# Loading the keys and queries of granule 5 ahead of the values of granule 4

## Chip, cores and metric

One core of one Trainium2 chip. The metric is device time in microseconds (us) of one execution, lower is better. A profile's span is about 1.8 us shorter than the time of the same execution. The runs of the kernel before that were known at the start spread over 0.57 us (208.49 to 209.06).

## The reference

Attention (4 batches, 8 heads, 768 positions, head size 64; each query sees 8 global keys and the last 96) followed by a two-layer block with a squared ReLU:

```python
scores = q @ k.T / sqrt(D) + bias;  a = softmax(where(keep, scores, -1e9))
x = (a @ v) -> (3072, 512)
out = (s * relu(x @ w_in)**2 + b) @ w_out        # d_ff = 2048
```

Keys, queries and values come in float32. The kernel works in bf16.

## The kernel before

The work is cut into 12 granules of 256 positions, three to a batch. A granule goes through loads, transposes of keys and queries, scores, exponential and mask, the value product, and the two layers. From granule 4 on the transposes are DMA transposes, issued by SyncE; the float32 loads, which cast to bf16, are issued by GpSimd (but for the first few of the opening). In the cuts below, the lines that work out `b`, `g` and `sb` are left out too.

```python
def load_qk(j, i):                      # block i: one load of keys, one of queries
    for n in range(2):
        nc.gpsimd.dma_start(nat_tile(j)[:, n, i, :, :], rows_of(srcs[n], b, g * GB + i))

def load_v(j, blocks=range(GB)):
    for i in blocks:
        nc.gpsimd.dma_start(vbuf[b % 2][:, sb, :, 0:D], rows_of(v, b, sb))
...
def qk_by_dma(j):                       # 4 transposes: block 0 keys, queries, block 1 keys, queries
    for i in range(GB):
        for n in range(2):
            nc.sync.dma_start_transpose(qk_of(b, n)[:, g * GB + i], nat[j][:, n, i, :, :]...)
...
warm(9, 4 * P)                          # opening: idle matmuls, so that TensorE's clock rises
...
warm(4)
qk_first(1, 0, cp)
...
    for i in range(GB):
        load_qk(4, i)
    load_v(3)
    load_v(4)
    load_granule(5)                     # k, q, k, q, v, v
...
qk_by_dma(4)
load_scalars()                          # two tiny loads, also on SyncE
...
qk_by_dma(5)
...
make_voff(4)                            # VectorE: reads values of 3 and block 0 of 4
...
step(8, [lambda: rest(2, 0)] + late_p1(3, (0,)), late_p1(3, (1, 2)), late_p1(3, (3,)))
step(9, p2[2][1:2], late_p1(3, (4, 5)), late_p1(3, (6, 7)))   # begins with granule 5's first scores
```

The softmax here doesn't subtract the row's maximum and nothing guards it: scores larger than these inputs give would overflow.

## Time and profile before

| | kernel before |
|---|---|
| time, first three runs | 208.49, 208.91, 209.06 us |
| time of the profiled execution | 209.15 us |
| span of the profile | 207.4 us |
| TensorE busy | 202.1 us (97%) |

With TensorE busy for 97% of the span, its own waits are the place to look.

### The profile page before, as it was taken

What the parts mean: (1) busy time and instruction counts of PE and PEld (TensorE: products, weight loads), DVE (VectorE), ACT (ScalarE), POOL (GpSimd) and SP (SyncE); (2) the same over time, 40 slices, a digit from 0 to 9 for tenths busy, and PEclk for the clock granted to TensorE, in tenths of its full rate; (3) what the DMA queues carried; (4) which work ended last, traced back from release to release, by engine and by line L of the source; (5) the groups of instructions that cost most, each with busy time, mean ns of one, the idle gap of its engine ahead of it and who ended that gap; (6) DMA issues with size and microseconds to landing.
All of it is one profiled execution on the core that took longest, in us unless ns stands there. A gap on an engine that the chain in (4) does not pass through costs nothing.

```text
span 207.4 us, 5323 instructions
## 1 busy us (share of the span) xinstructions
PE 202.1 (97%) x2191; PEld 160.1 (77%) x2191; DVE 161.3 (78%) x338; ACT 128.5 (62%) x198; POOL 68.9 (33%) x90
## 2 busy tenths in 40 slices
PE   7999999999999999999999999999999999999993
PEld 2678884557867485878888898888888889888883
DVE  7786599977989856799799974699866696737974
ACT  5875669486976548786664595663695764476200
POOL 8985333799365300810900828200000000000000
PEclk9999999999999999999999999999999999999999
DMA  5999999999999999999999999999570300240006
GB/s 164 172 179 202 207 206 177 155 152 129 110 150 120 151 132 218 155 213 212 152 198 153 125 154 178 194 172 126 52 206 0 95 14 0 56 150 0 0 9 196
DMA packets 110836, 28.17 MB, mean 136 GB/s; under 512 B 97852, under 2 KB 109308, under 8 KB 110812
## 3 DMA queue, kind: packets, MB, share of 16 engines
q0 software_dynamic: 76000, 13.11, 90.1%
q1 hardware_dynamic: 33612, 14.13, 41.7%
q10 hardware_dynamic: 1200, 0.59, 1.1%
q8 instruction: 17, 0.28, 0.6%
q14 instruction: 7, 0.06, 0.1%
HBM read 27.26 MB, written 6.29 MB: 162 GB/s over the span
## 4 chain that ended last, share of the span: by engine, by line
PE 65%; DMA 23%; POOL 9%; issue 1%; DVE 0%; POOLq 0%
PE ps L619 29%; PE ps L819 24%; DMA nat<-in_q_dram 12%; DMA w_in_bf<-in_moe_w_in_dram 6%; PE ps L667 5%; DMA qx<-nat 4%; PE ps_s L441 4%; PE ps_av L495 3%; POOL vb L108 3%; POOL nat L102 3%; POOL w_in_bf L140 2%; POOL nat L116 1%; PE ps_last L819 0%; DVE o_last L828 0%; POOL rel L173 0%
## 5 line engine op out<-in xcount | busy, mean ns | idle before, releaser
L619 PE MATMUL ps<-xT,w_in_bf 128*128 128x256 bf16 x768 | 90.3, 273 | 0.0
L629 ACT ACTIVATE gT<-ps 128x512 bf16<-128x512 f32 x96 | 55.8, 599 | 46.8 <-PE ps L619 46.6
L619 PEld LDWEIGHTS <-w_in_bf 128*128 128x128 bf16 x768 | 73.0, 98 | 9.4 <-DVE xT L594 0.2
L450 ACT ACTIVATE pt<-ps_s 128x1024 bf16<-128x1024 f32 (+1 forms) x44 | 39.3, 946 | 3.3 <-PE ps_s L441 3.3
L667 PE MATMUL ps<-w_out_bf,gT 128*128 128x512 bf16 x128 | 29.7, 380 | 0.0
L457 DVE TENSOR_TENSOR pt<-pt,tmpl 128x1024 bf16<-128x1024 bf16 (+1 forms) x40 | 24.6, 645 | 3.8 <-ACT pt L450 3.7
L819 PEld LDWEIGHTS <-gsum 128*128 128x128 bf16 x256 | 24.1, 98 | 3.7 <-DVE gsum L782 0.5
L108 POOL DMA_DIRECT2D vb<-in_v_dram x24 | 21.4, 906 | 6.9 <-DMA w_out_bf<-in_moe_w_out_dram 3.4
L793 DVE TENSOR_TENSOR gT<-gT 128x1024 bf16<-128x1024 bf16 x20 | 13.7, 686 | 11.7 <-ACT gT L629 11.7
L667 PEld LDWEIGHTS <-gT 128*128 128x128 bf16 x128 | 11.7, 98 | 13.0
L466 DVE TENSOR_TENSOR xn<-ps_av,rc 128x256 bf16<-128x256 f32 x48 | 20.4, 425 | 1.7
L819 PEld LDWEIGHTS <-gT 128*128 128x128 bf16 x200 | 18.6, 98 | 2.3
L465 DVE RECIPROCAL rc<-ps_av 128x4 f32<-128x4 f32 x48 | 8.6, 179 | 12.3 <-PE ps_av L495 10.4
L116 POOL DMA_DIRECT2D nat<-in_k_dram x16 | 14.2, 885 | 9.2 <-DMA nat<-in_k_dram 5.1
L495 PEld LDWEIGHTS <-pt 128*128 128x128 bf16 x320 | 14.4, 97 | 2.7 <-DVE xn L466 0.7
L632 DVE TENSOR_TENSOR gT<-gT 128x512 bf16<-128x512 bf16 x32 | 13.0, 422 | 3.5 <-ACT gT L629 3.3
L495 PE MATMUL ps_av<-vb,pt 128*128 128x65 bf16 x208 | 15.5, 193 | 0.0
L819 PE MATMUL ps<-w_out_bf,gsum 128*128 128x256 bf16 x128 | 15.3, 273 | 0.0
L116 POOL DMA_DIRECT2D nat<-in_q_dram x16 | 14.2, 888 | 2.9 <-DMA w_in_bf<-in_moe_w_in_dram 1.9
L819 PE MATMUL ps<-wsub,gsum 128*128 128x256 bf16 x128 | 15.1, 273 | 0.0
L819 PE MATMUL ps<-w_out_bf,gT 128*128 128x256 bf16 x120 | 13.9, 273 | 0.0
L122 POOL COPY gate<-xT 1x1 bf16<-1x1 bf16 x6 | 1.1, 176 | 35.9 <-DMA xT<-xn 35.9
(112 smaller groups left out, 228.5 us busy)
## 6 DMA issues: line engine op xcount, KB each, us to landing
out_dram<-o_q SPq DMA_DIRECT2D x15, 256.0 KB, 2.6
vb<-in_v_dram POOLq DMA_DIRECT2D x24, 128.0 KB, 8.3
nat<-in_k_dram POOLq DMA_DIRECT2D x22, 128.0 KB, 7.7
nat<-in_q_dram POOLq DMA_DIRECT2D x22, 128.0 KB, 7.6
w_out_bf<-in_moe_w_out_dram POOLq DMA_DIRECT2D x4, 512.0 KB, 16.2
w_in_bf<-in_moe_w_in_dram POOLq DMA_DIRECT2D x4, 256.0 KB, 7.4
w_in_bf<-in_moe_w_in_dram POOLq DMA_DIRECT2D x2, 512.0 KB, 11.3
out_dram<-o_sb SPq DMA_DIRECT2D x4, 256.0 KB, 6.3
```

The costliest lines, as they stand in the source:

```text
L108: nc.gpsimd.dma_start(vbuf[b % 2][:, sb, :, 0:D], rows_of(v, b, sb))
L116: nc.gpsimd.dma_start(t[:, n, i, :, :], rows_of(srcs[n], b, sb))
L450: nc.scalar.activation(pt[:, :, 0:ncol], ps[:, :, 0:ncol], ACT.Exp, scale=QSCALE)
L457: nc.vector.tensor_tensor(pv, pv, m.rearrange("p h a c -> p h (a c)"), ALU.mult)
L466: nc.vector.tensor_tensor(dst, av[:, :, :, 0:D], rc[:].to_broadcast((P, 2, 2, D)), ALU.mult)
L495: nc.tensor.matmul(av[:, i, hi, 0 : D + 1], lhsT=pt[:, hi, c * P : (c + 1) * P], rhs=vv, start=(n == 0), stop=(n == len(terms) - 1),)
L619: nc.tensor.matmul(ps[:, i, :], lhsT=w_in_bf[:, kc, fc * P : (fc + 1) * P], rhs=xT[j][:, kc, :], start=(kc == 0), stop=(kc == KC - 1),)
L629: nc.scalar.activation(gs, ps[:], ACT.Relu)
L632: nc.vector.tensor_tensor(gs, gs, gs, ALU.mult)
L667: nc.tensor.matmul(po[:], lhsT=g_of(j)[:, fc, tb * P : (tb + 1) * P], rhs=w_out_bf[:, fc, :], start=(fc == 0), stop=(fc == FC - 1),)
L793: outs.append(lambda: nc.vector.tensor_tensor(gs, gs, gs, ALU.mult))
L819: nc.tensor.matmul(ps[:, tb, cs], lhsT=stat[:, fc, tb * P : (tb + 1) * P], rhs=mov[:, fc, cs], start=(fc == 0), stop=(fc == NH - 1),)
```

## The change

Intent: granule 5's keys and queries need a DMA transpose after their load, the values of granule 4 do not. So let the loads with the longer way go first. The number of loads and their sizes are the same.

```diff
     for i in range(GB):
         load_qk(4, i)
     load_v(3)
+    for i in range(GB):
+        load_qk(5, i)
     load_v(4)
-    load_granule(5)
+    load_v(5)
```

## The prediction

> **What bounds the kernel now.** I read the page first: which engine is full, and what the chain that ended last consists of.
>
> ```profile
> PE 202.1 (97%) x2191; PEld 160.1 (77%) x2191; DVE 161.3 (78%) x338; ACT 128.5 (62%) x198; POOL 68.9 (33%) x90
> PE 65%; DMA 23%; POOL 9%; issue 1%; DVE 0%; POOLq 0%
> ```
>
> TensorE has work for 202.1 of the 207.4 us span. The chain is TensorE in its last part and transfers in its first. I therefore asked what TensorE itself waited for in the whole execution. Two answers came, one of them in the opening:
>
> ```profile
> PE ps_w L161 <- DVE idle L151: 1.2, 1, 1.2
> PE ps_s L441 <- DMA qx<-nat: 0.5, 1, 0.5
> ```
>
> So one wait on a transfer exists after the opening, 0.5 us long. The chain in order of time says where it is:
>
> ```profile
> 48.56 11.61 DMA nat<-in_q_dram
> 60.17 0.02 issue
> 60.19 8.86 DMA qx<-nat
> 69.06 0.04 issue
> 69.10 0.57 PE ps_s L441 x14
> 69.66 3.56 PE ps L667 x16
> ```
>
> Read it downwards: a load of queries issued at 48.56 lands at 60.17. At once a DMA transpose of that block is issued. It lands at 69.06, and the score matmuls start 0.04 us later. From there to 204 us the chain is TensorE without a transfer. By the program's order these are the scores of the first two units of granule 5: scores(8) and scores(9), of granule 4, stand at 59.06 and 62.00, and each later step issues the next. The load is the last of the four that granule 5's keys and queries need, its query block 1.
>
> TensorE's timeline sizes the stall:
>
> ```profile
> 68.36 0.23 PE L441 MATMUL ps_s<-qx,kx 64*128 64x128 bf16 x2
> 69.10 0.34 PE L441 MATMUL ps_s<-qx,kx 64*128 64x128 bf16 x6 [0.51 <-DMA qx<-nat]
> 69.26 0.40 PE L441 MATMUL ps_s<-qx,ko 64*128 64x128 bf16 x8
> 69.60 3.63 PE L667 MATMUL ps<-w_out_bf,gT 128*128 128x512 bf16 x16
> ```
>
> Two score matmuls (block 0) run at 68.36, then nothing until block 1 is there. From the first of these 16 matmuls to the next group is 69.60 - 68.36 = 1.24 us. The same 16 undisturbed, of the next step, go from 77.13 to 77.69: 0.56 us. The stall is really 1.24 - 0.56 = 0.68 us; the 0.51 is less because the second matmul's modelled end is counted into the busy time.
>
> The order of the loads is seen in GpSimd's timeline:
>
> ```profile
> 42.35 3.51 POOL L108 DMA_DIRECT2D vb<-in_v_dram  x4
> 45.87 0.89 POOL L116 DMA_DIRECT2D nat<-in_k_dram  x1
> 46.74 0.89 POOL L116 DMA_DIRECT2D nat<-in_q_dram  x1
> 47.61 0.90 POOL L116 DMA_DIRECT2D nat<-in_k_dram  x1
> 48.56 0.88 POOL L116 DMA_DIRECT2D nat<-in_q_dram  x1
> 49.43 1.77 POOL L108 DMA_DIRECT2D vb<-in_v_dram  x2
> ```
>
> The four at 42.35 are the values of granules 3 and 4, then come keys and queries of 5, then its values. Issue plus time to landing, read for each issue alone, gives: values of 4 at 44.08 + 6.0 = 50.1 and 44.95 + 7.0 = 52.0; granule 5's keys and queries at 55.9, 57.3, 58.0 and 60.2.
>
> **What the Trainium skill says.** "DMA: Bandwidth & Descriptors", section "Queues, rings and completion order": an engine consumes a ring's descriptors in ring order, and goes round-robin between queues. The loads above do land in the order of issue, so a load moved forward should take the landing slot of the one it passes. The same page, "Issuing engines are not separate DMA queues": transfers issued from all engines interleave on the same 16. The trace agrees: from 55 to 59 us and from 60.5 to 68 us the transposes share with the loads, at 145 and 132 GB/s for both together. "Perfetto Trace Analysis", section "DMA Instruction — SWDGE (GPSIMD)": the profiled window of such an issue is descriptor generation, not the movement. Here it is 0.88 us against 6 to 14 us to landing, so what counts is the landing slot and not the 2 x 0.88 us of issue. The same page, "Tensor Engine Instruction (MATMUL, LD_WEIGHTS)": matmul ends are estimated, which is why I size the stall from starts.
>
> **The change part by part.** Nothing is added or removed: 14 loads of 128 KB stay, four of them pass two others. Issue work and bytes are equal.
>
> *Keys and queries of 5 go forward by two slots.* In the old slots the four would land at 50.1, 52.0, 55.9 and 57.3 instead of 55.9, 57.3, 58.0 and 60.2. SyncE issues their transposes in program order, after those of granule 4 and two small loads, the second of which runs from 52.08 to 53.57:
>
> ```profile
> 52.08 1.49 SPq L168 DMA_DIRECT2D b_bc<-in_moe_b_dram  x1
> 55.92 1.20 SPq L360 DMA_TRANSPOSE kx<-nat  x1
> 57.32 1.19 SPq L360 DMA_TRANSPOSE qx<-nat  x1
> 58.61 1.35 SPq L360 DMA_TRANSPOSE kx<-nat  x1
> 60.19 1.54 SPq L360 DMA_TRANSPOSE qx<-nat  x1
> ```
>
> Each of the four now waits for its load. With the change the first can go at 53.6 (held by SyncE, no longer by its load), the second at 54.9, the third at 56.2, the fourth at about 57.6 (its load lands at 57.3). The fourth is 60.2 - 57.6 = 2.6 us earlier. With 8.9 us to landing it would land at 66.5. Granule 4's last transpose lands at 49.41 + 9.7 = 59.1, and transposes go through in order; so I allow a further 0.5 to 1 us and say 66.5 to 67.5. TensorE asks at about 68.4. The stall of 0.68 us goes, and the rest of the 2.6 us is slack.
>
> *Values of 4 go back by four slots.* Their new slots are 58.0 and 60.2, perhaps 1 to 1.5 us later, as transposes will now run beside loads in 59 to 60.5, where loads had the engines alone. That makes about 59 and 61.5. The first reader of block 0 is VectorE's copy into the off-diagonal values at 62.31, of block 1 the value matmuls at 65.16. Slack is about 3 us for each, so this costs nothing.
>
> *What follows.* From 69.1 on everything TensorE does moves forward by what the stall gives up. The next transfers it needs are granule 6's transposes, issued 65.37 to 70.70, with the known landings at 73.9 and 77.6; their scores are due at 81.8 and would then be due at 81.1. Loads behind the reordered group keep their slots. I find no wait to give the time back.
>
> Sum: -0.68 us at most, -0.6 expected. 208.91 - 0.6 = 208.3 us.
>
> **The rivals.**
> 1. *The stall moves to granule 4.* Its last transpose lands at 59.1 and TensorE starts scores(8) at 59.06, so that one has no slack. If granule 5's transposes, issued 2.3 us earlier, slow it by half a microsecond, the gain is lost there: 208.8. For it: both share the engines with loads. Against it: granule 4's are issued by 51.4, ahead in the same queue. I give it 1 in 5.
> 2. *The transposes are bound by themselves.* If granule 5's cannot start until 60 us for a reason other than their issue, the landing stays at 69 and the time at 208.9. For it: latency of 8.4 to 9.7 us is far above 1.2 us of issue, so something queues. Against it: the first of granule 6 took some 7 us with the same load, and granule 5's issue is plainly bound by its loads. 1 in 8.
> 3. *The values of 4 come late.* If the landing slips beyond 62.3, VectorE stalls, its masks come later, and the value matmuls at 65.16 may too; a slip of 4 us would cost about 0.5 us, 209.3 or so. 3 us of slack speak against it. 1 in 20.
> 4. *More is gained than the stall.* TensorE is without a gap afterwards, so no.
>
> **Range and chances.** The three runs of before spread by 208.49 to 209.06, 0.6 us, as much as the gain. With rival 1 or 2 above and a good run below, 207.8 to 208.9 should hold 8 in 10. A gain of over 2% would be 4.2 us, six times the only stall to be had; a loss of that size would need several transfers to miss their users by microseconds. Both are near nothing.
>
> **What would show it.** In the changed profile, TensorE's wait on the transposed queries should be gone, the 16 score matmuls near 68.4 should take 0.56 us, the four transposes of 5 should start near 53.6, and the copy of the off-diagonal values should not wait for a load. I am wrong if a wait of TensorE stands at 59 us, if one remains near 68.4, or if VectorE waits for the values of granule 4. Then the chain would again show a transfer just ahead of TensorE, at another place.

## The result, and the profile after

| | before | after |
|---|---|---|
| median of the same rounds | 208.72 us (208.49 to 209.06, 4 runs) | 208.81 us (208.60 to 208.93, 4 runs) |
| ratio | | 1.0002 (0.9983 to 1.0021) |
| span of the profile | 207.4 us | 207.1 us |

A ratio is the mean time of one kernel's fast runs over that of the other's of the same rounds, so not quite the ratio of the medians quoted. The result is inside the range of the prediction, near its upper end; the gain of 0.6 us is not there.

The wait itself is gone. All waits of TensorE in the profile after:

```profile
PE ps_w L161 <- DVE idle L151: 1.2, 1, 1.2
PE ps_s L441 <- ACT qx L331: 0.3, 1, 0.3
PE ps L667 <- issue: 0.2, 1, 0.2
```

None is for a transfer. TensorE's timeline after, at granule 5's first scores:

```profile
68.83 0.40 PE L441 MATMUL ps_s<-qx,kx 64*128 64x128 bf16 x8
69.06 0.39 PE L441 MATMUL ps_s<-qx,ko 64*128 64x128 bf16 x8
69.38 3.63 PE L667 MATMUL ps<-w_out_bf,gT 128*128 128x512 bf16 x15
```

The 16 score matmuls take 69.38 - 68.83 = 0.55 us, as predicted, where they took 1.24 us. But they begin at 68.83 and not at 68.36: TensorE is 0.47 us late when it gets there. So the next group starts only 69.60 - 69.38 = 0.22 us earlier than before, and the spans differ by about as much (207.1 against 207.4 us).

How the loads moved, from GpSimd's timeline after:

```profile
42.06 1.77 POOL L108 DMA_DIRECT2D vb<-in_v_dram  x2
43.79 0.91 POOL L102 DMA_DIRECT2D nat<-in_k_dram  x1
44.66 0.92 POOL L102 DMA_DIRECT2D nat<-in_q_dram  x1
45.52 0.94 POOL L102 DMA_DIRECT2D nat<-in_k_dram  x1
46.40 0.94 POOL L102 DMA_DIRECT2D nat<-in_q_dram  x1
47.26 3.61 POOL L108 DMA_DIRECT2D vb<-in_v_dram  x4
```

With the times to landing of these issues (6.0, 6.8, 7.6 and 10.3 us), keys and queries of 5 land at 49.8, 51.5, 53.1 and 56.7 us; the two value loads of granule 4 land at 47.26 + 10.2 = 57.5 and 48.24 + 11.2 = 59.4. SyncE's timeline after shows the transposes of granule 5:

```profile
52.41 2.27 SPq L360 DMA_TRANSPOSE kx<-nat  x1
54.78 1.22 SPq L360 DMA_TRANSPOSE qx<-nat  x1
56.10 1.32 SPq L360 DMA_TRANSPOSE kx<-nat  x1
57.52 2.05 SPq L360 DMA_TRANSPOSE qx<-nat  x1
```

The last lands 8.9 us after its issue, at 66.4, which is 2.4 us ahead of the matmuls.

Where, then, were the 0.47 us lost? Ahead of anything that the change touches, in the opening. TensorE's timeline of the kernel before, and then that of the changed one, at the first four bias matmuls:

```profile
5.85 0.81 PE L416 MATMUL ps_s<-open_bf 128*128 128x384 bf16 x4
```

```profile
6.13 1.32 PE L416 MATMUL ps_s<-open_bf 128*128 128x384 bf16 x4
```

These are the same four matmuls at the same place, before any load of granule 4 or 5 is issued: 0.81 us in one execution and 1.32 in the other. The traces' records of the granted clock explain it: full speed begins at 5.14 us in the one and at 7.15 us in the other. The page's clock row shows tenths of full speed in slices of 5 us and has 9 from its first slice in both, so one does not see it there. The Trainium skill, "TensorE: Matmul & The Clock Gate", section "What's actually happening", says that the clock rises after some 3.4 us of activity, counted in a free-running window, and is therefore "run-variable". The traces agree that it varies: in eleven further ones below, all of kernels with these nine idle matmuls, the rise is between 4.0 and 6.8 us. With TensorE's first matmul at 1.2 us, the earliest rise came after 2.8 us of work, not 3.4.

At its scores near 9 us the changed kernel is 9.55 - 8.86 = 0.69 us behind. The kernel before then loses some 0.2 us of that lead on the way to 68 us, 0.1 of it at scores(8), which take 59.73 - 59.06 = 0.67 us there and 0.56 in the changed kernel.

So two things were open. Is the 0.68 us of the wait a property of the kernel, or of the one execution that was profiled? And does the opening only hide the gain, or was there none?

### The profile page after: what moved, and what is told of

It is laid out like the page before. It is cut to its first block, busy times and chain, and to the rows that moved or that the text cites. A ratio compares the mean times of both kernels' runs of the same rounds, so it can differ in the third digit from the quotient of the medians.

```text
span 207.1 us, 5315 instructions
## 1 busy us (share of the span) xinstructions
PE 201.7 (97%) x2183; PEld 160.3 (77%) x2191; DVE 160.7 (78%) x338; ACT 128.4 (62%) x198; POOL 69.7 (34%) x90
## 4 chain that ended last, share of the span: by engine, by line
PE 95%; DMA 2%; DVE 1%; issue 0%; ACT 0%
PE ps L619 41%; PE ps L819 24%; PE ps L667 13%; PE ps_s L441 6%; PE ps_av L495 5%; DMA first<-in_k_dram 2%; PE ps_t L351 1%; PE ps_s L517 1%; PE ps_t L327 1%; PE ps_x L591 1%; PE ps_s L416 1%; PE ps_s L532 1%; PE ps_av L558 1%; PE ps_t L341 0%; PE ps_last L819 0%
## 5 line engine op out<-in xcount | busy, mean ns | idle before, releaser
L667 PE MATMUL ps<-w_out_bf,gT 128*128 128x512 bf16 x120 | 28.7, 380 | 0.5 <-issue 0.2
L116 POOL DMA_DIRECT2D nat<-in_q_dram x14 | 12.5, 890 | 6.8 <-DMA nat<-in_q_dram 2.8
L116 POOL DMA_DIRECT2D nat<-in_k_dram x14 | 12.4, 884 | 5.8 <-DMA w_in_bf<-in_moe_w_in_dram 2.4
```

The costliest lines, as they stand in the source:

```text
L116: nc.gpsimd.dma_start(t[:, n, i, :, :], rows_of(srcs[n], b, sb))
L667: nc.tensor.matmul(po[:], lhsT=g_of(j)[:, fc, tb * P : (tb + 1) * P], rhs=w_out_bf[:, fc, :], start=(fc == 0), stop=(fc == FC - 1),)
```

## The experiments

**Theory A**: the wait is in most executions of the kernel before, the change removes it, and the moment of the clock hides it. **Theory B**: the wait belonged to one late landing, and most executions have none. **Theory C**: the time comes back at a later wait. The later expectations sharpen B to **theory B'**: the time is set by when TensorE asks for the last transposed query (when it gets to granule 5's first scores), plus what the landing is behind this ask; and in most executions of the kernel before, the landing is ahead of it. Theory D there is that the landing does not matter. All were timed with five rounds, four kernels at a time on one chip, another chip for each four.

**The kernel before, again.**

> Control: the kernel before, unchanged, against itself. Theory A (the stall is real and gone after the change; the gain is hidden because TensorE's clock reaches full speed at another moment of the opening in every execution, 5.1 us in the profile of before and 7.2 us in that of after): ratio 1.000 within 0.001; in its profile the wait for the transposed queries of granule 5 is between 0 and 0.7 us, the smaller the later the clock rises (about 0.7 us for a rise by 5.3 us, about 0.1 us for a rise at 7 us or later). Theory B (the 0.68 us stall belonged to that one execution: a late landing): no such wait here although the clock rises early. Theory C (the stall is gone after the change but the time comes back at a later place): says nothing here but that the stall is there.

Measured: ratio 1.0000 (0.9988 to 1.0012), span 206.7 us. TensorE's timeline:

```profile
68.41 0.40 PE L441 MATMUL ps_s<-qx,kx 64*128 64x128 bf16 x8
68.64 0.39 PE L441 MATMUL ps_s<-qx,ko 64*128 64x128 bf16 x8
68.96 3.63 PE L667 MATMUL ps<-w_out_bf,gT 128*128 128x512 bf16 x15
```

The same program asks at the same time (68.41 against 68.36), and the 16 matmuls take 0.55 us: no wait. The clock rose at 4.09 us, so theory A's rule, early rise and long wait, fails here. SyncE's timeline of this run shows why the landing was in time:

```profile
53.26 1.60 SPq L360 DMA_TRANSPOSE kx<-nat  x1
56.90 1.19 SPq L360 DMA_TRANSPOSE qx<-nat  x1
58.18 1.30 SPq L360 DMA_TRANSPOSE kx<-nat  x1
59.58 1.25 SPq L360 DMA_TRANSPOSE qx<-nat  x1
```

The first key load of granule 5 landed 7.5 us after its issue at 45.74, and not 10.0 us; the last query load at 59.2 and not 60.2; the last transpose at 59.58 + 8.3 = 67.9 us and not 69.1. That is half a microsecond ahead of the ask. Two more traces have the loads in this order, of the two versions of the kernel before in which only TensorE's work is moved (further below): their last transposes land at 67.8 and 68.7 us. So the four landings (67.8, 67.9, 68.7, 69.1) scatter by more than a microsecond, on both sides of an ask at 68.4; the first profile has the latest of them.

The record also shows what the first key load met. The traffic of the core's DMA engines in the first profile, from 40 to 56 us, each figure 0.4 us:

```profile
GB/s 154 155 154 156 152 157 150 157 152 157 169 146 149 155 145 142 146 137 151 143 152 156 160 96 45 46 148 122 133 165 117 128 2 8 10 136 143 160 151 146
```

From 52.8 to 54.0 us nearly nothing moves, while this load is under way. In the second profile such a hole begins only at 54.5, and the load had landed at 53.2. In twelve of the fourteen traces of this document there is a stretch of 0.8 us with 5 to 19 GB/s between 52.8 and 55.6 us, 1.0 to 1.7 us after a 16 KB transfer on the DMA queue that the profile names "instruction". What causes it is not shown, nor how much of the later landing of the last transpose comes from it.

**The changed kernel, again**, three times.

> The changed kernel again, to narrow the interval. Theory A: ratio to before 0.998 to 0.9995 (0.1 to 0.4 us less); no wait of TensorE on transposed queries, whenever the clock rises; the span of the profile is about 206.5 us for an early rise and 207.1 us for a late one. Theory B: ratio 1.000 within 0.0005. Theory C: ratio 1.000, and a wait of TensorE after 70 us that the kernel before does not have.

Measured: 1.0002 (0.9990 to 1.0015), above the 0.998 to 0.9995 of theory A, though the interval takes in the upper part of these; span 206.8 us, rise of the clock at 6.2 us, no wait for a transposed query.

> The changed kernel a third time, for the tail. Theory B': the runs of the kernel before have a tail over 209.0 us (4 of 31 so far, the executions whose landing comes late), the changed kernel has none (0 of 9 so far); means equal within 0.15 us, ratio 0.999 to 1.0005. If the changed kernel has the same tail, it comes from something other than this wait.

Measured: 1.0004 (0.9992 to 1.0016), no run over 209.0 us.

> The changed kernel a fourth time, for the same count: theory B' expects no run over 209.0 us, ratio 0.999 to 1.0005.

Measured: 1.0015 (1.0000 to 1.0030), outside the expected range, and one run at 209.38 us, a miss. All runs of the two kernels taken together, over all blocks: before 42 runs, mean 208.62, median 208.51 us; after 20 runs, mean 208.70, median 208.70. Over 209.0 us are 5 of 42 and 1 of 20. So a tail that the change cuts off is not shown; and a gain of 0.2 us or more in the mean, as theory A has it, is not there.

**Half of the change.**

```diff
     load_v(3)
-    load_v(4)
-    load_granule(5)
+    load_v(4, [0])
+    for i in range(GB):
+        load_qk(5, i)
+    load_v(4, [1])
+    load_v(5)
```

> Half of the change: keys and queries of granule 5 pass only one of the two value loads of granule 4. Theory A (landing slots decide): the transposes of granule 5 are issued about 1.3 us earlier than before, the last lands at about 67.5 to 68 us, just ahead of the scores at 68.4: little or no wait left, time within 0.2 us of the changed kernel. Theory B: the same time as before and after, no wait in any.

Measured: 1.0006 (0.9994 to 1.0018); the last transpose was issued at 58.01 and landed at 65.8 us, earlier than expected; there was no wait. The time is that of before and of after.

**The other way round**: one slot and two slots later than before.

```diff
-    load_granule(5)                    # one slot later
+    load_v(5, [0])
+    for i in range(GB):
+        load_qk(5, i)
+    load_v(5, [1])
```

```diff
-    load_granule(5)                    # two slots later
+    load_v(5)
+    for i in range(GB):
+        load_qk(5, i)
```

> Keys and queries of granule 5 one slot later than before: one of the two loads of granule 5's values goes ahead of them. With the last transpose landing at 66.4 to 66.8 us two slots earlier, 65.8 one slot earlier, 67.9 to 69.1 in the old place and 70.8 two slots later, theory B' (time = when TensorE asks, plus what the landing is behind it) expects a landing at 69 to 70 us, a wait of 0.6 to 1.5 us and a time 0.5 to 1.3 us over before (ratio 1.0025 to 1.006). A theory in which the landing does not matter expects no change.

> The change turned round: keys and queries of granule 5 come after its values, two slots later than before. Theory A: their last transpose lands some 2 to 3 us later, at 71 to 72 us, TensorE waits 2.5 to 3.5 us there, and the time is 1.5 to 2.8 us more than before (ratio 1.008 to 1.013). Theory B (that landing does not matter in most executions): under 1 us more. If the transposes were bound by themselves and not by their loads, no change at all.

Measured: 1.0056 (1.0030 to 1.0081) and 1.0127 (1.0091 to 1.0164). TensorE's timeline with one slot, and with two:

```profile
68.70 0.23 PE L441 MATMUL ps_s<-qx,kx 64*128 64x128 bf16 x2
70.22 0.34 PE L441 MATMUL ps_s<-qx,kx 64*128 64x128 bf16 x6 [1.29 <-DMA qx<-nat]
```

```profile
68.13 0.23 PE L441 MATMUL ps_s<-qx,kx 64*128 64x128 bf16 x2
70.83 0.34 PE L441 MATMUL ps_s<-qx,kx 64*128 64x128 bf16 x6 [2.46 <-DMA qx<-nat]
```

This is the shape of the prediction's profile, two matmuls and then a hole, and here the time follows. One run of the six with one slot was at 208.46 us, as fast as the kernel before. That fits a landing that scatters, but there is no trace of this run. Two of the six with two slots took 212.1 and 212.6 us, with a mean clock of 0.992 where the others have 0.997 to 1.0; I have no trace of those two. The other four are at 210.2 to 210.8 and alone would make the ratio about 1.009.

Put side by side, the kernels form one scale, but for the half, which landed earliest (slots against before; issue of the last transpose plus its time to landing; start of the first score matmul; time to the next group, 0.55 without a wait; ratio of times):

| kernel | slots | last landing | scores start | to next group | span | ratio |
|---|---|---|---|---|---|---|
| after, first profile | 2 earlier | 66.4 | 68.83 | 0.55 | 207.1 | 1.0002 |
| after, second | 2 earlier | 66.8 | 68.51 | 0.55 | 206.8 | 1.0002 |
| after, third | 2 earlier | 66.3 | 68.62 | 0.59 | 207.0 | 1.0004 |
| after, fourth | 2 earlier | 66.7 | 68.24 | 0.55 | 206.6 | 1.0015 |
| half | 1 earlier | 65.8 | 68.65 | 0.55 | 207.0 | 1.0006 |
| before, second | 0 | 67.9 | 68.41 | 0.55 | 206.7 | 1.0000 |
| before, first | 0 | 69.1 | 68.36 | 1.24 | 207.4 | |
| one slot later | 1 later | 70.2 | 68.70 | 2.02 | 208.5 | 1.0056 |
| two slots later | 2 later | 70.8 | 68.13 | 3.20 | 209.1 | 1.0127 |

Adding start and time to the next group and taking the sum from the span leaves 137.7 to 137.8 us in every row: in these executions nothing after granule 5's first scores differs. That excludes theory C. What they took was decided by when TensorE got to these scores, plus what the landing was behind.

This also gives an estimate for the executions without a trace. The median of the 42 runs before, 208.51 us, less 1.78 (time over span, the mean of all runs), 137.75 and 0.55, leaves 68.43 us for the start and the wait together. The earliest start in the table is 68.13. So in half of the runs the wait was at most some 0.3 us, and a wait of 0.68 us is not the usual case.

**Using up the reserve on TensorE's side.** One group of 8 matmuls is moved from ahead of these scores to behind them, in both kernels; the work is the same.

```diff
-    step(8, ..., late_p1(3, (1, 2)), late_p1(3, (3,)))
-    step(9, p2[2][1:2], late_p1(3, (4, 5)), late_p1(3, (6, 7)))
+    step(8, ..., late_p1(3, (1, 2)), [])
+    step(9, p2[2][1:2], late_p1(3, (3, 4, 5)), late_p1(3, (6, 7)))
```

> The kernel before, with one group of 8 projection matmuls (0.87 us of TensorE work) moved from ahead of granule 5's first scores to behind them: TensorE asks for the transposed queries at about 67.5 instead of 68.4 us, all else equal. Theory B' (in most executions of the kernel before the last transpose of granule 5 lands at about 67.9 us, half a microsecond ahead of the ask, so the change removes a wait that is seldom there): now the wait is in nearly every execution, 0.4 to 1.5 us, and the time is 0.3 to 1.0 us more than before (ratio 1.0015 to 1.005). Theory A (the wait is there in most executions anyhow): the wait grows by 0.87 us and the time by about 0.85 us. Theory D (the landing does not matter at all): no change.

> The same move of 8 matmuls in the changed kernel. Its last transpose lands at 66.4 to 66.8 us, ahead of an ask at 67.5: no wait, ratio to before 0.999 to 1.0005, under theories A and B' alike. So the pair differs by 0.3 to 1.0 us under B', which is the worth of the change once its slack is used; by nothing under D. If there is a wait at the scores of granule 6 (near 81.7 us), whose loads land 1 to 2 us later in the changed kernel, it shows here.

Measured: 1.0029 (1.0004 to 1.0053) and 1.0015 (0.9996 to 1.0034). TensorE's timeline of the first:

```profile
67.33 0.23 PE L441 MATMUL ps_s<-qx,kx 64*128 64x128 bf16 x2
67.79 0.34 PE L441 MATMUL ps_s<-qx,kx 64*128 64x128 bf16 x6 [0.23 <-DMA qx<-nat]
```

And of the changed kernel with the same move:

```profile
67.47 0.40 PE L441 MATMUL ps_s<-qx,kx 64*128 64x128 bf16 x8
68.07 0.40 PE L441 MATMUL ps_s<-qx,ko 64*128 64x128 bf16 x8 [0.21 <-DVE rc L465]
```

The wait for the transpose is in the one and not in the other, as B' expects. But the second has a wait that I did not expect, and its ratio is above the expected 0.999 to 1.0005, a miss. The view names a reciprocal on VectorE; what these matmuls read is the copy of the off-diagonal keys (ko), which ended at the same moment, 68.02 us. In the first trace it ended at 67.63, so this wait too may belong to one execution. The difference of the pair, 0.14% or 0.3 us, has the right sign and the lower end of the expected size, and the intervals overlap. That the change would pay if TensorE came earlier is not shown by this pair.

**Making TensorE later.** Six more idle matmuls in the opening of both kernels.

```diff
-    warm(4)
+    warm(10)
     qk_first(1, 0, cp)
```

> The kernel before with six more idle matmuls (0.64 us) on TensorE in the opening, so that everything of TensorE, the ask at 68.4 too, comes 0.6 us later. Theory A (a wait of about 0.7 us in most executions): the wait takes it up and the time grows by under 0.2 us. Theory B' (no wait in most): the time grows by 0.5 to 0.65 us, ratio 1.0024 to 1.0031, and no wait is seen.

> The same six idle matmuls in the changed kernel. No wait to take them up under any theory: the time grows by 0.5 to 0.65 us over the changed kernel, ratio to before 1.0024 to 1.0035. Under theory A this pair differs by 0.4 us or more, under B' by under 0.2 us.

Measured: 1.0018 (0.9997 to 1.0039) and 1.0022 (1.0003 to 1.0041), or 0.4 and 0.5 us by 208.5. Both are below the 0.5 to 0.65 us expected, but each interval reaches 0.4 us to either side. The pair differs by about 0.1 us, where theory A wanted 0.4 or more: this speaks against a wait in most executions that would take a delay up, but with such intervals it does not exclude one. Neither profile has a wait. In that of before the landing (68.74) is only just ahead of the delayed ask (68.86); at the usual 68.4 it would have been late.

**Without the warm-up.** The changed kernel without its first nine idle matmuls:

```diff
-    warm(9, 4 * P)
     cast_first(0, 0, cp)
```

> The changed kernel without the nine idle matmuls at its start. TensorE then begins at about 5.2 us, the full clock is granted not at 4 to 7 us but some 4 us later (8 to 11 us), and the matmuls between run at half speed. If the moment of the full clock is what spreads the runs of both kernels over 206.5 to 207.1 us of span, the ask at 68.4 and the end both move by about the same amount, 0.7 to 2.5 us, ratio 1.003 to 1.012. If the opening is bound by loads and casts and not by TensorE's speed, the time stays within 0.3 us.

Measured: 1.0084 (1.0071 to 1.0097). Full speed begins at 11.15 us, the scores of granule 5 start at 70.25, without a wait, and the span is 208.5 us. So a later rise of the clock moves everything behind it. It accounts for the direction of the spread (rises at 6.2 to 7.2 us went with starts at 68.5 to 68.8). The scores near 9 us show it best: with rises at 5.2, 5.7, 6.2, 6.7 and 7.2 us (qk5_last, the changed kernel's fourth, second, third and first profiles) they begin at 8.77, 8.96, 9.17, 9.36 and 9.55. But it is not all: two profiles with a rise at 4.1 us begin them at 8.97 and 9.04, and granule 5's scores at 68.7 and 68.4. In these two TensorE waits 0.6 us for a cast ahead of its first transposes. What else is in it I leave open.

No version was found that beats both kernels. Outside the opening, no profile of the changed kernel has a wait of TensorE over 0.2 us left.

## Why the prediction was right or wrong

- **TensorE bounds the kernel, and the one wait on a transfer is for granule 5's last query block.** Right for the execution that was profiled.
- **A load moved forward takes the landing slot of the one it passes.** Right for three of the four: 49.8, 51.5, 53.1 and 56.7 us against 50.1, 52.0, 55.9 and 57.3 forecast. The third slot was 2.8 us earlier, since the forecast took over the late landing of the one profile (55.9, beside the hole in the traffic); in the second profile of the kernel before the same slot is 53.2. The passage that the prediction cites for ring order stands in a paragraph on the queues of SyncE and ScalarE, and it adds that completion need not follow the order of issue. What carries the argument is the traces: in all fourteen the loads near 40 to 56 us land in the order of issue.
- **The transposes start at 53.6, 54.9, 56.2 and 57.6 and the last lands at 66.5 to 67.5.** Right within 0.1 us but for the first: 52.4, 54.8, 56.1, 57.5, landing 66.4. The first went 1.2 us earlier, as the second small load ahead of it took 0.63 us and not 1.49. (The 7 us that rival 2 gives for the first transpose of granule 6 are those of its second, 66.73 to 73.9; the first one's landing is not in the trace.)
- **The values of granule 4 have slack.** Right: they land at 57.5 and 59.4, and VectorE's copy at 62.86 waits for nothing. Rivals 1 and 3 did not happen: the 16 matmuls of scores(8) take 60.20 - 59.64 = 0.56 us, and the lists of waits have nothing there.
- **Loads behind the group keep their slots.** Not quite: granule 6's first key load lands at 66.0 us and not 65.2. Whether the earlier transposes do that is not shown; between the four traces with the old order the same landing varies from 64.3 to 65.2. It cost nothing: its scores have no wait in any profile.
- **"Sum: -0.68 us at most, -0.6 expected."** This is the step that failed. The 0.68 us were measured correctly, but in one execution, and taken as the kernel's own. In the second profile the same wait is 0. Landings scatter by 1.3 us around the ask (67.8, 67.9, 68.7 and 69.1 in four traces, against 68.4), and the ask itself moves by 0.7 us with the opening; the prediction took both as fixed. The mean of 42 runs before is 0.08 us below that of 20 after, and the standard error of that difference is 0.07 us (standard deviations 0.29 and 0.25), so the average gain is too small for these runs to show, under some 0.1 us against 0.6 forecast.
- **The range.** It held (208.81 in 207.8 to 208.9), as I had set the upper end by the spread of the runs and two rivals. Neither rival happened; the reason that the result lies near that end is one that I did not list, so that it held is luck as far as the mechanism goes: the range also holds the time of the kernel before. There was a hint beforehand: the profiled execution took 209.15 us, 0.66 us over the fastest of the three others, which is the size of the wait. It was no more than a hint, as another of the three took 209.06.

Open: how often the kernel before has the wait, what makes the holes in the DMA traffic, and what else makes the last landing late. Also open is whether the higher median after (208.70 against 208.51 us) is anything: four of the changed kernel's four profiles have the clock rise at 5.7 us or later and both of the kernel before at 5.2 or earlier, but I know of no way in which the order of loads at 43 us could reach back to that. The variants do not keep it up: the two with before's order rise at 4.1 and 5.6, the two with the changed order at 4.0 and 6.4.

## What to carry to other kernels

A wait that one trace shows is one draw. If it is as long as the spread of the runs, compare the time of the profiled execution with the others, or take a second trace, before counting on it. Moving loads forward by landing slots works as reckoned, but it pays only where the landing is usually behind the ask; here one slot too late costs 1.2 us, and one or two slots early earn reserve, but no time that these runs can show.

## What the Trainium skill lacked or had wrong

- "DMA: Bandwidth & Descriptors", "Anatomy of one DMA — SWDGE (gpsimd) path", gives 2.0 us plus bytes over 436 GB/s for one DMA, an estimate of 2.3 us for 128 KB. With up to eight casting loads in the queue and transposes beside them, these took 6.0 to 14.7 us to landing in the changed kernel's first profile. The page has no figure for a load in a full queue.
- No page says how much a landing scatters between executions of the same program: the same transpose landed at 67.9 and 69.1 us in two executions of one program, the load that began the delay 7.5 and 10.0 us after its issue.
- No page tells of holes in a core's DMA traffic like those above: 5 to 19 GB/s over 0.8 us in twelve of fourteen traces, where 120 to 170 are usual.
- No page gives the time of one DMA transpose beside loads: 7.8 to 9.1 us from issue to landing for the last block of granule 5 (128 x 512 bf16) in the rows of the table. "DMA: Bandwidth & Descriptors", "Latency and other measured facts", gives only bandwidths, 261 GB/s and some 350 to 400 for the contiguous case.
- "TensorE: Matmul & The Clock Gate", "What's actually happening", is right that the start of full speed varies between runs, but gives ±500 ns for it. It was 4.0 to 7.2 us here with TensorE's work starting at 1.2 us, so 2.8 to 6.0 us of work. The window itself shows in the traces: full speed lasts 201.39 or 204.80 us in them, 59 or 60 times 3.413 (197.97, 58 times, without the warm-up). Its advice not to fit to a count holds, but that the spread can be as large as the gain of a small change (the scores near 9 us start at 8.77 to 9.55 us) is worth a warning there.
